# Spatial mixing by 26 block products of 4x4 blocks instead of seven of 2x2 blocks

## The chip, the cores and the metric

The kernel runs on one core of a Trainium2 chip. The metric is the device time of one execution in microseconds (us). Five engines work side by side, each in the order in which its instructions were written: PE multiplies matrices, DVE works on vectors, ACT applies functions and copies, POOL is a second, slower vector engine, and SP issues most of the DMAs (ACT issues those of the output). The profile adds PEld, the loading of PE's stationary operand, which overlaps PE.

## The reference, cut to what matters

One transformer block of 2048 tokens (S) and 448 channels (D): attention with 16 heads, then a gated MLP whose gate mixes the tokens. All data is float32.

```
h = layernorm(x) * (1 + ca) + sa
x = x + ga * attention(h)                 # 16 heads of 28 channels
h = layernorm(x) * (1 + cb) + sb
z = gelu(h @ w_in)                        # 2048 x 1792
z1 = z[:, :896]
z2 = layernorm(z[:, 896:])
g[t, f] = sum_s w_sp[t, s] * z2[s, f] + b_sp[t]     # the spatial mixing, 2048 x 2048 by 2048 x 896
x = x + gb * ((z1 * g) @ w_out)           # w_out: 896 x 448
```

The change concerns the line of `g`, and what prepares and consumes it.

## The kernel before

**Numbers and tiles.** A float32 matrix product is made of three matmuls in the format fp32r: each operand is split into a high part (an ACT copy) and a low part (a DVE subtraction), and high times high, high times low and low times high are summed in PSUM. In the mixing the stationary operand is a piece of z2 (128 tokens by 128 channels) and the moving one a piece of the transposed weights `w_spT` (128 source tokens by 512 target tokens). The 896 channels are seven tiles of 128, numbered f = 0 to 6. A matmul fills one PSUM bank with 128 channels by 512 targets.

**The mixing** (main loop L1420 to L1439). Targets, sources and channels 0 to 767 are halved, so that the mixing is a 2x2 by 2x2 block product, and it is done with seven block products instead of eight, at the price of sums of blocks. Two products make one phase, so there are four phases `p` (the last holds one product); each has two halves of the targets of a product, and each half eight steps `st` of 128 sources, which makes 64 steps. `mix_step` (matmuls L1250 to L1252) issues in one step three channel tiles of the first product, three of the second and the seventh channel tile, into seven of the PSUM ring's banks, where the sums grow over the eight steps of a half. `evac` then reads all seven banks, by ACT copies where an output is written first (L1262, L1275, L1282) and by DVE additions through `d_add` (L1255).

**Sums of weight blocks** come early. During attention 80 slots of its schedule (L818 to L825) hold the loading of two blocks by SP (`ws_load`), their sum on POOL (`ws_add`, L791) and its store to DRAM (`ws_store`, into `ws_scr`). Attention goes through 256 units of a head and a block of queries; slot n stands before unit n. In attention POOL also multiplies the heads' outputs by reciprocals of the softmax sums (L710) and prepares row maxima (L648, L649, L84), which PE transposes (`mtp`, L655).

**Sums of z2** are made by `z_sum` (L1143), some on POOL, some on DVE. The parts of the stationary operands are split per source tile by `prep0` to `prep3` (L1146 to L1162, L1227), into `heapA` and `heapB`.

**Order around it.** Nothing reorders instructions: the main loop writes them, and each engine takes its own in that order. `w_load` (L1125) fetches a weight tile some steps ahead into a pool of four buffers (`raw_sp`), `w_split` (L1133) splits it one or two steps ahead (`wsp_h` by ACT at L1138, `wsp_l` by DVE at L84). `extras` (L1364) lays the rest into the steps: the z parts, then `gate` (L1311: DVE adds the bias and multiplies by z1), `u_split` (L1322, the gated output into high and low parts `uT`), and the weights of the output projection (`wout_gate`, `wout_part`). `y_part` (L1350, matmuls L1356 to L1358) is the projection: 16 tiles of 128 tokens with 21 matmuls each. Tiles 8 to 11 stand inside the last half, tiles 12 to 15 and 0 to 7 behind the mixing. Before all this, `z2_gemm` (L1170) computes z2 tile by tile.

L84 before, and L141 after, is the line of the helper `sub`, which makes every low part on DVE or POOL.

Of the kernel before, what the change touches and what calls it, by code (L numbers as in the profile page):

```python
# [19 lines left out]
NT = S // 128  # L20
NG = 4

# [11 lines left out]
def tile_adaln_mha_gmlp(ctx, tc, x, wqkv, wo, w_in, w_spT, b_sp, w_out, cT, w_mod, out):  # L34
# [13 lines left out]
    ws_scr = scr.tile([80, 128, 512], F32, name="ws_scr")  # L48
# [22 lines left out]
    class Halves:  # L71
# [5 lines left out]
        def __getitem__(self, key):  # L77
            p, b, c = key
            return self.views[b // self.n][p, b % self.n, c]
# [675 lines left out]
    def win_first(i):  # L755
# [9 lines left out]
    SUMS = (  # L765
        ((0, 1), (1, 1), ALU.subtract),
        ((1, 0), (0, 0), ALU.subtract),
        ((0, 0), (1, 1), ALU.add),
        ((0, 0), (0, 1), ALU.add),
        ((1, 0), (1, 1), ALU.add),  # L770
    )

    def w_block(rc, st, half):
        rb, cb = rc
        return w_spT[(rb * 8 + st) * 128 : (rb * 8 + st + 1) * 128, (2 * cb + half) * 512 : (2 * cb + half + 1) * 512]
# [3 lines left out]
    def ws_tiles(i):  # L779
        if not ws_raw:  # L780
            ws_raw.append(dpool.tile([128, 7, 512], F32, name="ws_raw", tag="heapF"))
        return [ws_raw[0][:, 2 * (i % 3) + j, :] for j in range(2)]

    def ws_load(i):
        k, j = divmod(i, 16)
        for t, rc in zip(ws_tiles(i), SUMS[k]):
            sp.dma_start(t, w_block(rc, j // 2, j % 2))

    def ws_add(i):
        a, b = ws_tiles(i)  # L790
        pool.tensor_tensor(out=a, in0=a, in1=b, op=SUMS[i // 16][2])  # L791

    def ws_store(i):
        sp.dma_start(ws_scr[i], ws_tiles(i)[0])
# [116 lines left out]
    heapA = fh.tile([128, 8 * 896], F32R, name="heapA")  # L911
    heapB = fh.tile([128, 8 * 896], F32R, name="heapB")
    xl3 = fh.tile([128, 7, 512], F32, name="xl3", tag="heapC")
    w1 = hview(heapA, 0, 8, 896)
    h2T = [hview(heapB, g * 3584, 7, 512) for g in range(2)]

    zst = [(heapA, heapB)[i // 4][:, i % 4 * 1792 : (i % 4 + 1) * 1792] for i in range(8)]
# [185 lines left out]

    wp = ctx.enter_context(tc.tile_pool(name="wp", bufs=4))  # L1110
    F1, F2, F6, FQ = slice(0, 384), slice(384, 768), slice(768, 896), slice(384, 896)

    PHASES = (("s", 0, (1, 1)), ("s", 1, (0, 0)), ("s", 2, 3), ("s", 4, None))
    steps = [(p, half, st) for p in range(4) for half in range(2) for st in range(8)]

    def w_sources(p, half, st):
        _, k, q = PHASES[p]
        res = [ws_scr[k * 16 + st * 2 + half]]
        if q is not None:
            res.append(ws_scr[q * 16 + st * 2 + half] if isinstance(q, int) else w_block(q, st, half))  # L1120
        return res[::-1] if p == 3 else res

    raws, wsp = {}, {}

    def w_load(n):  # L1125
        if n < len(steps) and n not in raws and n not in wsp:
            raws[n] = []
            for src in w_sources(*steps[n]):
                t = wp.tile([128, 512], F32, name="raw_sp")
                sp.dma_start(t, src)  # L1130
                raws[n].append(t)

    def w_split(n):  # L1133
        if n < len(steps) and n not in wsp:
            wsp[n] = []
            for raw in raws.pop(n):
                hi = wp.tile([128, 512], F32R, name="wsp_h")
                act.activation(hi, raw, AF.Copy)  # L1138
                lo = wp.tile([128, 512], F32R, name="wsp_l")
                sub(dve, lo, raw, hi)  # L1140
                wsp[n].append((hi, lo))

    def z_sum(dst, a, b, op=ALU.add, eng=pool):  # L1143
        eng.tensor_tensor(out=dst, in0=a, in1=b, op=op)

    def z_part(hi, lo, src):  # L1146
        act.activation(hi, src, AF.Copy)
        sub(dve, lo, src, hi)

    def prep0(st):  # L1150
        h, l = zst[st][:, 0:896], zst[st][:, 896:1792]
        z_part(h[:, F1], l[:, F1], z2[st][:, F1])
        z_part(h[:, F2], l[:, F2], z2[8 + st][:, F1])
        z_part(h[:, F6], l[:, F6], z2[8 + st][:, F6])

    def prep1(st):
        h, l = zst[st][:, 0:896], zst[st][:, 896:1792]
        z_part(h[:, F1], l[:, F1], z2[8 + st][:, F2])
        z_part(h[:, FQ], l[:, FQ], z2[st][:, FQ])

    def prep2(st):
        z_part(zst[st][:, 0:896], zst[st][:, 896:1792], z2[st])  # L1162

    zt = [dpool.tile([128, 8 * 896], F32, name=f"z2{i}", tag=f"heapD{i}") for i in range(2)]
    z2 = [zt[i // 8][:, i % 8 * FH : (i % 8 + 1) * FH] for i in range(NT)]
    ph4 = ExitStack()
# [20 lines left out]
    def z2_norm(t):  # L1187
        mv, rs = z_mv.pop(t)
        dve.tensor_scalar(out=z2[t], in0=z2[t], scalar1=mv[:, 0:1], scalar2=rs, op0=ALU.subtract, op1=ALU.mult)
        if t >= 8:  # L1190
            z_sum(z2[t][:, F1], z2[t][:, F1], z2[t - 8][:, F1])

    for t in range(NT + 1):
        if t < NT:
            z2_gemm(t)
        if 0 < t <= NT:
            z2_norm(t - 1)
        if t in (10, 11, 14, 16):
            w_load((10, 11, 14, 16).index(t))
        if t in (13, 15):  # L1200
            w_split(t // 15)
        if 10 <= t < NT:
            prep0(t - 10)
# [4 lines left out]
    cE = fh.tile([128, 4 * 896], F32, name="cE", tag="heapE")  # L1208
    cC = fh.tile([128, 4 * 896], F32, name="cC", tag="heapC")
    cF = dpool.tile([128, 4 * 896], F32, name="cF", tag="heapF")  # L1210
    cD = dpool.tile([128, 4 * 896], F32, name="cD", tag="heapD2")
    u11, u12, u21, u22 = ([c[:, i * 512 : (i + 1) * 512] for i in range(6)] for c in (cE, cC, cF, cD))

    dq = [c[:, 3072:3584] for c in (cE, cC)]
    u6 = [c[:, 3072:3584] for c in (cF, cD)]

    def utile(f, tb):
        if f == 6:
            return (dq, u6)[tb // 2][tb % 2]
        return ((u11, u12), (u21, u22))[f // 3][tb // 2][2 * (f % 3) + tb % 2]  # L1220

    wouts_h, wouts_l = (hview(heapB, i * 3136, 7, D) for i in range(2))
    z7l = t4.tile([128, 256], F32R, name="z7l", bufs=1)
    z7 = [(heapA[:, i * 1024 : i * 1024 + 768], heapA[:, i * 1024 + 768 : i * 1024 + 1024]) for i in range(7)]
    z7.append((heapB[:, 6272:7040], z7l))

    def prep3(st):  # L1227
        a, b = z7[st]
        z_part(a[:, 0:384], a[:, 384:768], z2[8 + st][:, F1])
        z_part(b[:, 0:128], b[:, 128:256], z2[8 + st][:, F6])  # L1230

    def stationary(p, st, i):

        if p < 3:
            return zst[st][:, i * 128 : (i + 1) * 128], zst[st][:, 896 + i * 128 : 896 + (i + 1) * 128]
        a, b = z7[st]
        if i < 3:
            return a[:, i * 128 : (i + 1) * 128], a[:, 384 + i * 128 : 384 + (i + 1) * 128]
        return b[:, 0:128], b[:, 128:256]

    acc = {}

    def mix_step(n):
        p, half, st = steps[n]
        for i in (range(7) if p < 3 else (0, 1, 2, 6)):
            if st == 0:
                acc[i] = bank("acc")
            hi, lo = wsp[n][0 if i < 3 else -1]
            zh, zl = stationary(p, st, i)
            pe.matmul(acc[i], zh, hi, start=st == 0, stop=False)  # L1250
            pe.matmul(acc[i], zh, lo, start=False, stop=False)  # L1251
            pe.matmul(acc[i], zl, hi, start=False, stop=st == 7)  # L1252
        del wsp[n]

    def d_add(dst, a, b, op=ALU.add):  # L1255
        dve.tensor_tensor(out=dst, in0=a, in1=b, op=op)  # L1256

    def evac(p, x):
        for f in range(3):
            i = 2 * f + x  # L1260
            if p == 0:
                act.activation(u22[i], acc[f], AF.Copy)  # L1262
            elif p == 1:
                act.activation(u21[i], acc[f], AF.Copy)
                d_add(u11[i], u11[i], acc[f])
            elif p == 2:
                d_add(u11[i], u11[i], acc[f])
                d_add(u22[i], u22[i], acc[f])
            else:
                d_add(u11[i], u11[i], acc[f])  # L1270
        for f in range(3):
            i = 2 * f + x
            if p == 0:
                d_add(u12[i], u22[i], acc[3 + f])
                act.activation(u11[i], acc[3 + f], AF.Copy, scale=-1.0)  # L1275
            elif p == 1:
                d_add(u21[i], u21[i], acc[3 + f])
                d_add(u22[i], u22[i], acc[3 + f], ALU.subtract)
# [208 lines left out]
```

## Time and profile before

| what | us |
|---|---|
| median of 3 runs (1395.46 to 1396.77) | 1396.19 |
| span of the profiled execution | 1394.6 |
| up to the mixing (start of its first matmul) | 1050.3 |
| mixing and output projection | 344.3 |
| DVE busy in attention's window (170 to 975) | 629.1 of 805 |
| DVE, ACT and POOL busy in the last 344.3 us | 217.7, 120.6, 32.7 |

The three runs' median is 1.6 us above the span of the execution that was profiled; stages and durations are from that execution. The window from 170 to 975 us holds attention and the projections up to z1, that from 975 to 1050.3 the product that gives z2. A row of a window lists its length and then, for each engine, busy time and the number of instructions; a row of the groups lists line, engine, operation, output and inputs, their shapes, the count, the busy time, the mean duration in ns, and the idle time of that engine ahead of them with what ended it. A row of the timeline gives start, duration, engine, line, operation, and in square brackets how long it waited and for what.

### The profile page before, as it was taken

How to read it: one execution, taken by the hardware profiler on the slowest of the kernel's cores; microseconds unless marked ns; L12 is line 12 of the kernel's file. 1: busy time of each engine (PE TensorE's matmuls, PEld its weight loads, DVE VectorE, ACT ScalarE, POOL GpSimd, SP SyncE). 2: the span in 40 equal slices, each digit the busy share in tenths (PEclk: the TensorE clock that was granted, in tenths of full speed). 3: DMA queues.
4: the chain of work that ended last, by engine and by line, in shares of the span. 5: the costliest groups of instructions: out<-in, count | busy, mean ns of one | idle time of the engine just before them, and what ended most of it. 6: DMA issues, size and time to landing. Idle time of an engine off the chain costs nothing.

```text
span 1394.6 us, 20350 instructions
## 1 busy us (share of the span) xinstructions
PE 1389.6 (100%) x7192; PEld 991.3 (71%) x7192; DVE 1028.3 (74%) x1741; ACT 777.0 (56%) x1490; POOL 282.7 (20%) x306
## 2 busy tenths in 40 slices
PE   9999999999999999999999999999999999999999
PEld 8888655555555555555555555988998888888888
DVE  8798888888888888888888851850366655768574
ACT  5623677777766666777777779363234544434211
POOL 2234212222224143313200021000142330000000
PEclk9999999999999999999999999999999999999999
DMA  8565634555455546555322002433103333444453
GB/s 266 149 178 181 192 109 152 175 173 155 149 173 175 158 161 184 167 158 153 113 68 76 21 18 68 166 123 139 48 4 111 112 110 111 143 137 163 142 171 113
DMA packets 99377, 187.01 MB, mean 134 GB/s; under 512 B 17736, under 2 KB 29130, under 8 KB 96730
## 3 DMA queue, kind: packets, MB, share of 16 engines
q1 hardware_dynamic: 96558, 181.42, 42.4%
q10 hardware_dynamic: 2718, 4.30, 0.8%
q8 instruction: 56, 0.92, 0.3%
q14 instruction: 45, 0.37, 0.1%
HBM read 130.42 MB, written 50.46 MB: 130 GB/s over the span
## 4 chain that ended last, share of the span: by engine, by line
PE 99%; DMA 0%; DVE 0%; ACT 0%; ACTq 0%; issue 0%
PE st_ps L666 19%; PE o_ps L681 17%; PE mt L634 17%; PE acc L1250 7%; PE acc L1252 7%; PE acc L1251 7%; PE z_ps L1176 5%; PE pq L323 5%; PE z_ps L1062 5%; PE wo_ps L928 3%; PE pv L305 2%; PE y_ps L1357 2%; PE y_ps L1358 2%; PE y_ps L1356 2%; PE tp L117 1%; PE pv L477 1%
## 5 line engine op out<-in xcount | busy, mean ns | idle before, releaser
L639 DVE TENSOR_REDUCE pm<-mt 128x1 f32<-128x512 f32 x1024 | 631.3, 682 | 86.0 <-PE mt L634 85.9
L670 ACT ACTIVATE P<-st_ps 128x512 f32<-128x512 f32 x1024 | 514.7, 632 | 201.8 <-PE st_ps L666 201.7
L666 PE MATMUL st_ps<-qst,kst 128*128 128x512 f32 x1024 | 404.5, 406 | 0.0
L634 PE MATMUL mt<-kst,qst 128*128 128x512 f32 x1024 | 402.4, 393 | 0.0
L666 PEld LDWEIGHTS st_ps<-qst,kst 128*128 128x128 f32 x1024 | 191.2, 188 | 141.4 <-issue 93.1
L681 PE MATMUL o_ps<-P,V 128*32 128x512 f32 x2048 | 247.1, 598 | 0.0
L634 PEld LDWEIGHTS mt<-kst,qst 128*128 128x128 f32 x1024 | 192.4, 188 | 31.6
L791 POOL TENSOR_TENSOR ws_raw<-ws_raw 128x512 f32<-128x512 f32 x80 | 102.9, 1287 | 298.5 <-DMA ws_raw<-in_w_spT_dram 295.7
L1138 ACT ACTIVATE wsp_h<-raw_sp 128x512 fp32r<-128x512 f32 x112 | 70.0, 631 | 153.6 <-PE acc L1252 102.4
L681 PEld LDWEIGHTS o_ps<-P,V 128*32 128x32 f32 x2048 | 54.7, 109 | 123.0 <-issue 114.7
L84 DVE TENSOR_TENSOR wsp_l<-raw_sp,wsp_h 128x512 fp32r<-128x512 f32 x112 | 80.6, 729 | 81.9 <-ACT wsp_h L1138 81.2
L1250 PE MATMUL acc<-wsp_h,heapA 128*128 128x512 f32 x224 | 87.3, 390 | 0.0
L1251 PE MATMUL acc<-wsp_l,heapA 128*128 128x512 f32 x224 | 87.2, 389 | 0.0
L1252 PE MATMUL acc<-wsp_h,heapA 128*128 128x512 f32 x224 | 87.2, 389 | 0.0
L1251 PE MATMUL acc<-wsp_l,heapB 128*128 128x512 f32 x174 | 67.7, 389 | 0.0
L1250 PE MATMUL acc<-wsp_h,heapB 128*128 128x512 f32 x174 | 67.7, 389 | 0.0
L1252 PE MATMUL acc<-wsp_h,heapB 128*128 128x512 f32 x174 | 67.7, 389 | 0.0
L323 PE MATMUL pq<-heapD,heapD 128*128 128x512 f32 x196 | 61.9, 390 | 0.0
L1180 DVE BATCH_NORM_STATS2 stz<-z 128x6 f32<-128x448 f32 x32 | 19.9, 625 | 50.4 <-ACT z L1179 30.0
L1250 PEld LDWEIGHTS acc<-wsp_h,heapA 128*128 128x128 f32 x224 | 42.1, 188 | 8.9 <-DVE cD L1256 0.3
L1252 PEld LDWEIGHTS acc<-wsp_h,heapA 128*128 128x128 f32 x224 | 42.0, 188 | 8.8
L1251 PEld LDWEIGHTS acc<-wsp_l,heapA 128*128 128x128 f32 x224 | 42.0, 188 | 8.6
(224 smaller groups left out, 1598.8 us busy)
## 6 DMA issues: line engine op xcount, KB each, us to landing
ws_raw<-in_w_spT_dram SPq DMA_DIRECT2D x160, 256.0 KB
ws_scr<-ws_raw SPq DMA_DIRECT2D x80, 256.0 KB
raw_sp<-ws_scr SPq DMA_DIRECT2D x80, 256.0 KB
kst<-qk_scr SPq DMA_DIRECT2D x45, 224.0 KB
qst<-qk_scr SPq DMA_DIRECT2D x45, 224.0 KB
raw_sp<-in_w_spT_dram SPq DMA_DIRECT2D x32, 256.0 KB
qk_scr<-qh SPq DMA_DIRECT2D x28, 256.0 KB
qk_scr<-ql SPq DMA_DIRECT2D x28, 256.0 KB
```

The lines of the kernel that those rows point to most:

```text
L84: eng.tensor_tensor(out=dst, in0=a, in1=hi.bitcast(F32), op=ALU.subtract)
L323: pe.matmul(pq, wqk[:, b, m * 128 : (m + 1) * 128], hT[g][:, a, :], start=j == 0, stop=j == NST - 1)
L634: pe.matmul(mt, qst[h % 3][:, t * 128 : (t + 1) * 128], kst[h % 3][:, kb * 512 : (kb + 1) * 512], start=True, stop=True)
L639: dve.tensor_reduce(out=pms[h][:, t, kb : kb + 1], in_=mt, axis=AX.X, op=ALU.max)
L666: pe.matmul(st, kst[h % 3][:, kt * 128 : (kt + 1) * 128], qst[h % 3][:, qb * 512 : (qb + 1) * 512], start=True, stop=True)
L670: act.activation(p, st, AF.Exp, scale=SCALE)
L681: pe.matmul(otile[h][32 * qb : 32 * qb + 32, :], V[:, kt, h, :], ptiles.pop((u, qb)), start=kt == 0, stop=kt == NT - 1)
L791: pool.tensor_tensor(out=a, in0=a, in1=b, op=SUMS[i // 16][2])
L1138: act.activation(hi, raw, AF.Copy)
L1250: pe.matmul(acc[i], zh, hi, start=st == 0, stop=False)
L1251: pe.matmul(acc[i], zh, lo, start=False, stop=False)
L1252: pe.matmul(acc[i], zl, hi, start=False, stop=st == 7)
```

## The change

The mixing becomes 26 block products of 4x4 source and target blocks of 512 tokens. A product takes a combination of weight blocks (512 sources by 512 targets) and a combination of z2 blocks (512 sources by 384 channels), four steps of 128 sources. Three channel tiles belong to a product; the 768 channels are two blocks of three tiles (`A`: f = 3 to 5, `B`: f = 0 to 2), hence 2x4 by 4x4. The seventh tile (f = 6) rides with 16 of the products as a fourth tile. Each product's row in `PRODUCTS` says with which signs it enters the outputs (four blocks of targets of `A`, with f = 6, then four of `B`), whether f = 6 is in it, whether it starts a new chain, and which block of the weights it uses directly (`None`: a combination from `ws_scr`).

In a chain the PSUM banks are not cleared: a product is added to what its banks hold from the product before it in the same set. Products use the two sets (n even, n odd) in turn. After a product only those outputs read the running sum whose sign changes at that place (function `coef`); 28 reads write an output first and are ACT copies, 77 are DVE additions.

The sums of weights are listed in `W_SUMS`, slot by slot, with seven buffers: `0=w14.0` loads, `2=0+1` adds on POOL, `-2` negates on POOL, `p15.0=2` stores, `3=p20.0` loads a stored one again. There are 124 additions, 20 negations, 72 loads of weights, 12 of stored sums and 92 stores; before there were 80, 0, 160, 0 and 80. Sums of z2 move to DVE and take four source tiles in one instruction, as do the high parts (`z_hi`, ACT) and low parts (`z_low`, DVE). Bias and gate move from DVE to POOL, but for those written into `rest`. All 16 tiles of the output projection stand behind the mixing. Matmuls of the mixing: 1128 for 1200.

```diff
+PRODUCTS = [
+    ("0000000-", False, True, None),
+    ("0+0-0000", True, True, 1),
+    ("0000++-0", False, True, None),
+    ("-0+0+0-0", False, True, None),
+    ("0000+000", False, False, 0),
...
+W_SUMS = (
+    "2:0=w14.0,1=w13.0 3:3=w2.0 5:2=0+1,-2 6:4=w15.0,0=3-0,p15.0=2 7:5=w11.0,2=1-0,p14.0=0 8:p16.0=2 9:0=4+1 "
...
+    def ws_op(op):
+        if op[0] == "p":
...
+            sp.dma_start(ws_scr[4 * n + st], ws_tile(i))
+        elif op[0] == "-":
...
+            pool.tensor_scalar(out=t, in0=t, scalar1=-1.0, scalar2=None, op0=ALU.mult)
+        elif op[2] in "wp":
...
+            sp.dma_start(ws_tile(op[0]), w_block(n, st) if op[2] == "w" else ws_scr[4 * n + st])
+        else:
+            pool.tensor_tensor(
...
-    for i, slot in enumerate([j for j in range(2, 190, 2) if j % 16 != 12][:80]):
-        at(slot, ws_load, i)
-        at(slot + 3, ws_add, i)
-        at(slot + 5, ws_store, i)
+    for entry in W_SUMS.split():
...
-        at(200 + 8 * i, win_first, i)
+        at(204 + 8 * i, win_first, i)
...
+    def z_op(out, a, b, op=ALU.add):
+        dve.tensor_tensor(out=out, in0=a, in1=b, op=op)
...
+    def z_hi(n, *srcs):
...
+            act.activation(zhi[n % 3][:, :, c], s, AF.Copy)
...
+    def z_low(n):
+        for c, s in zsrc.pop(n):
+            sub(dve, zlo[n % 3][:, :, c], s, zhi[n % 3][:, :, c])
...
+    SUMS = {
+        4: lambda: [(ZS, ZA[0], ZB[2]), (ZS, ZS, ZB[0])],
+        5: lambda: [(ZS, ZA[0], ZT[0])],
...
+    def z_begin(n):
+        for s in SUMS[n]() if n in SUMS else ():
+            z_op(*s)
+        if n in HIS:
+            z_hi(n, *HIS[n]())
...
+    def mix_step(i):
+        n, st = mix[i]
...
+        for j in range(4 if six else 3):
+            start = st == 0 and (first6[n] if j == 3 else new)
...
+            for k, (z, w) in enumerate(((zh, hi), (zh, lo), (zl, hi))):
+                pe.matmul(
+                    a[j], z[:, c], w, start=start and k == 0, stop=st == 3 and k == 2, skip_group_check=not new or j == 3
...
+    def read(u, a, r, key):
+        if key not in written:
+            written.add(key)
+            act.activation(u, a, AF.Copy, scale=float(r))
+        else:
+            d_add(u, u, a, ALU.add if r > 0 else SUB)
...
+    def bias(f, k, eng=pool):
+        d_add(utile(f, k), utile(f, k), bt[k], eng=eng)
...
+    gates(20, 3, B3, 3, gate)
+    gates(21, 1, A4, 3, z1_load)
+    gates(22, 0, A4, 3, gate)
+    gates(22, 1, B3, 3, u_split)
...
+    for i, (n, st) in enumerate(mix):
+        w_load(i + 5)
+        w_load(i + 4)
+        w_split(i + 3 if i else 3)
+        if st == 0 and n:
+            todo += read_list(n - 1)
+        mix_step(i)
+        if st == 1:
+            z_begin(n + 2) if n + 2 not in (2,) else None
+        for _ in range(3):
+            if todo:
+                read(*todo.pop(0))
+        if st == 3:
+            z_end(n + 2) if n + 2 not in (2,) else None
+        for fn, a in extra.pop((n, st), []):
+            fn(*a)
...
+    last = [12, 13, 14, 15] + list(range(12))
...
+    for k, t in enumerate(last):
...
+        y_part(t)
+        for fn, *a in rest.get(k, ()):
+            fn(*a)
```

How the order of the instructions changes is shown at three places. First the reading of the banks. Before, on ACT at the end of the first half of phase 0, it stands in one piece; `cD` and `cE` are output buffers, `acc` a PSUM bank:

```order
L1262 ACTIVATE cD<-acc 128x512 x3
L1275 ACTIVATE cE<-acc 128x512 x3
L1282 ACTIVATE cE<-acc 128x512
L1138 ACTIVATE wsp_h<-raw_sp 128x512 x4
L1147 ACTIVATE heapA<-z_10937 128x384
```

After, on ACT in products 2 and 3, which read the banks of products 1 and 2; `cC` too is an output, `cE` here the sum of z2 blocks for product 4:

```order
L1409 ACTIVATE cC<-acc 128x512
L1409 ACTIVATE cD<-acc 128x512
L1409 ACTIVATE cC<-acc 128x512
L1170 ACTIVATE wsp_h<-raw_sp 128x512
L1203 ACTIVATE heapA<-cE 128x4x384
L1409 ACTIVATE cD<-acc 128x512
L1409 ACTIVATE cC<-acc 128x512
L1409 ACTIVATE cD<-acc 128x512
L1170 ACTIVATE wsp_h<-raw_sp 128x512
L1409 ACTIVATE cC<-acc_11625 128x512
L1409 ACTIVATE cD<-acc_11625 128x512
L1170 ACTIVATE wsp_h<-raw_sp 128x512 x2
```

The reads now stand in groups of up to three per step between the splits, and the high part of the z2 sum for the product after next (L1203) stands ahead of three to five of them.

Second, POOL in one head of attention. Before, from one row maximum to the next:

```order
L791 TENSOR_TENSOR ws_raw<-ws_raw 128x512 x5
L710 TENSOR_TENSOR osb<-osb,rb 128x512
L791 TENSOR_TENSOR ws_raw<-ws_raw 128x512 x2
L648 TENSOR_SCALAR mxv<-mxv 128x16
L649 CAST mxp<-mxv 128x16
```

After, a head in the same place of the program:

```order
L845 TENSOR_TENSOR ws_raw<-ws_raw 128x512 x4
L840 TENSOR_SCALAR ws_raw<-ws_raw 128x512
L845 TENSOR_TENSOR ws_raw<-ws_raw 128x512
L840 TENSOR_SCALAR ws_raw<-ws_raw 128x512
L845 TENSOR_TENSOR ws_raw<-ws_raw 128x512 x2
L767 TENSOR_TENSOR osb<-osb,rb 128x512
L845 TENSOR_TENSOR ws_raw<-ws_raw 128x512 x3
L705 TENSOR_SCALAR mxv<-mxv 128x16
```

Ten sums or negations stand where seven sums stood, and three instead of two of them between the normalisation (`osb`) and the row maximum (`mxv`).

Third, DVE and POOL in products 22 and 23, where nothing comparable stood before. DVE (`uT` is the split of gated outputs, `cE`, `cC` are outputs that read a bank):

```order
L1392 TENSOR_TENSOR cE<-cE,acc 128x512 x3
L141 TENSOR_TENSOR wsp_l<-raw_sp,wsp_h 128x512
L1193 TENSOR_TENSOR z_10936<-z_10936 128x4x384
L1392 TENSOR_TENSOR cE<-cE,acc_12874 128x512
L141 TENSOR_TENSOR uT<-cD,uT 128x512
L141 TENSOR_TENSOR wsp_l<-raw_sp,wsp_h 128x512
L141 TENSOR_TENSOR uT<-cD,uT 128x512
L141 TENSOR_TENSOR wsp_l<-raw_sp,wsp_h 128x512
L141 TENSOR_TENSOR heapA<-z_10936,heapA 128x4x384
```

POOL in the same stretch, where `bt` is a bias and the numbered `z` a tile of z1:

```order
L1392 TENSOR_TENSOR cD<-cD,z_13232 128x512
L1392 TENSOR_TENSOR cF<-cF,bt 128x512
L1392 TENSOR_TENSOR cD<-cD,z_13252 128x512
L1392 TENSOR_TENSOR cF<-cF,bt 128x512
L1392 TENSOR_TENSOR cD<-cD,z_13273 128x512
L1392 TENSOR_TENSOR cF<-cF,bt 128x512
```

The gates and biases that stood on DVE now stand on POOL, one or two for each step of the mixing.

More of the change, by code (lines that the diff above doesn't have):

```diff
@@ L1110, in tile_adaln_mha_gmlp @@
     wp = ctx.enter_context(tc.tile_pool(name="wp", bufs=4))
[L1111 to L1121, printed above, removed]
@@ L1123, in tile_adaln_mha_gmlp @@
-    raws, wsp = {}, {}
[L1125 to L1141, printed above, removed]
@@ L1209, in tile_adaln_mha_gmlp @@
[L1209 to L1220, printed above, removed]
@@ L1222, in tile_adaln_mha_gmlp @@
[L1222 to L1278, printed above, removed]
[L1279 to L1286 removed]
+    us += [fh.tile([128, 4 * 896], F32, name="cC", tag="heapC")]
@@ new lines, in zb, with d_add, read_list @@
+    def zb(n):
+        return 1 if n == NP - 1 else n % 3
+    def d_add(dst, a, b, op=ALU.add, eng=dve):
+        eng.tensor_tensor(out=dst, in0=a, in1=b, op=op)
+    written = set()
+    def read_list(n):
+        res = []
+        for j in range(4):
+            for o, r, six in reads[n]:
+                if six != (j == 3):
+                    continue
+                f, k = (3 + j if o < 4 else j), o % 4
+                res.append((utile(f, k), acc[n % 2][j], r, (f, k)))
+        return res
```

511 lines of the change are left out of this document (308 added, 203 removed).

## The prediction

> **What bounds the kernel now.** I read the page's busy times, its slices and its chain first, then the span cut into stages.
>
> ```profile
> span 1394.6 us, 20350 instructions
> ...
> PE 1389.6 (100%) x7192; PEld 991.3 (71%) x7192; DVE 1028.3 (74%) x1741; ACT 777.0 (56%) x1490; POOL 282.7 (20%) x306
> ...
> PEclk9999999999999999999999999999999999999999
> ...
> PE 99%; DMA 0%; DVE 0%; ACT 0%; ACTq 0%; issue 0%
> ```
>
> PE is on the chain for 99% of the span at full granted clock, so time can be won only by taking instructions from PE, and lost only by making it wait. But a busy share is a poor witness, because pipelined matmuls overlap. The stages, and two 20 us pieces of the spatial mixing, show it better:
>
> ```profile
> 170.00:975.00 805.00, 805.00 (x4445) 493.27 (x4445) 629.14 (x1081) 547.35 (x1067) 171.69 (x185) 1.00 0.44 132
> 1050.30:1394.60 344.30, 340.79 (x1537) 288.04 (x1535) 217.66 (x340) 120.61 (x215) 32.74 (x29) 1.00 0.41 132
> ...
> 1150.00:1170.00 20.00, 20.00 (x90) 16.54 (x90) 11.46 (x18) 7.23 (x12) 0.00 (x0) 1.00 0.28 90
> 1190.00:1210.00 20.00, 20.00 (x89) 16.29 (x88) 15.38 (x23) 8.96 (x15) 0.00 (x0) 1.00 0.48 144
> 1370.00:1394.60 24.60, 21.09 (x105) 19.20 (x103) 5.85 (x10) 1.19 (x3) 0.00 (x0) 1.00 0.25 84
> ```
>
> Columns after the window: its length, then busy time and count of PE, PEld, DVE, ACT and POOL, clock, DMA share, GB/s. The mixing and the output projection after it (second row) have only the 3.5 us tail in which PE is idle (24.60 less 21.09). The pace inside is read from the start of the first mixing matmul and that of the 673rd (phases 0 and 1 are 336 each), both in the timeline:
>
> ```profile
> 1050.30 0.39 PE L1250 MATMUL acc<-wsp_h,heapA 128*128 128x512 f32 x1
> ...
> 1202.63 0.39 PE L1250 MATMUL acc<-wsp_h,heapA 128*128 128x512 f32 x1
> ```
>
> 152.33 us over 672 is **0.2267 us a matmul**, without a gap. The 390 ns of a matmul's own duration is latency and prices nothing here.
>
> **The change part by part.** *Removed from PE.* Before: seven block products of 3 channel tiles, 16 steps and 3 matmuls (1008), and the seventh tile in four phases of 16 steps (192), 1200 in all. After: 26 x 3 x 4 x 3 = 936, and 16 x 4 x 3 = 192 for the seventh tile, 1128. 72 fewer at 0.2267 us: **-16.3 us**. The output projection keeps its 336 matmuls; 84 of them, tiles 8 to 11, move from inside phase 3 to behind the mixing, where tiles 12 to 15 come first, and their operands are finished in products 22 to 25. PE waited nowhere in this stretch but in its tail (above), so I cost the move at nothing.
>
> *Added beside PE.* A product has 36 or 48 matmuls, so 8.16 or 10.88 us (26 of them 255.7 us), in which the other engines must have split the weights, built the next product's stationary tiles and read the banks. Prices:
>
> ```profile
> L84 DVE TENSOR_TENSOR wsp_l<-raw_sp,wsp_h 128x512 fp32r<-128x512 f32 x112 | 80.6, 729 | 81.9 <-ACT wsp_h L1138 81.2
> L84 DVE TENSOR_TENSOR uT<-cD,uT 128x512 fp32r<-128x512 f32 x7 | 4.8, 684 | 0.0
> L84 DVE TENSOR_TENSOR heapA<-z,heapA 128x896 fp32r<-128x896 f32 x4 | 4.4, 1093 | 0.6
> L1144 DVE TENSOR_TENSOR z<-z,z 128x384 f32<-128x384 f32 x8 | 4.4, 550 | 0.0
> L1256 DVE TENSOR_TENSOR cE<-cE,acc 128x512 f32<-128x512 f32 x19 | 12.6, 683 | 0.9 <-PE acc L1252 0.9
> L1138 ACT ACTIVATE wsp_h<-raw_sp 128x512 fp32r<-128x512 f32 x112 | 70.0, 631 | 153.6 <-PE acc L1252 102.4 <-DVE x2t L1361 28.0 <-DMA raw_sp<-ws_scr 16.1
> L1147 ACT ACTIVATE heapA<-z 128x384 fp32r<-128x384 f32 x19 | 9.3, 511 | 0.0
> L1147 ACT ACTIVATE heapA<-z 128x896 fp32r<-128x896 f32 x4 | 3.8, 938 | 0.0
> L791 POOL TENSOR_TENSOR ws_raw<-ws_raw 128x512 f32<-128x512 f32 x80 | 102.9, 1287 | 298.5 <-DMA ws_raw<-in_w_spT_dram 295.7 <-PE mt L634 2.7
> ```
>
> The new z operations take 1536 or 2048 elements of a partition at once, which no row shows. From 384 (550 ns) to 896 elements (1093 ns) DVE adds 1.06 ns an element: 1.77 and 2.31 us, estimates. Bounds: one 896 operation, 1.09, from below, four of 384, 2.2, from above. ACT by its two rows: 1.47 and 1.90 us. I use these, being on the line through both rows. DVE then has 104 splits (71.1 at 684 ns), 73 reads of banks (49.9), z lows (47.5), z sums (38.8), uT and wouts (9.2): 217 us in 255.7, 85%. ACT has about 130. So no engine replaces PE on average; what counts is where the load bunches.
>
> *Bunch one, products 2 to 4.* The 28 first reads are ACT's, and products 1 and 2 have 14 of them. ACT runs in order, and the row of the z high part stands ahead of later reads and waits for sums on DVE. Reads out of PSUM on ACT come at 0.62 us each:
>
> ```profile
> 1087.35 1.96 ACT L1275 ACTIVATE cE<-acc 128x512 f32<-128x512 f32 x3 [0.87 <-DVE cC L1256]
> 1089.20 0.59 ACT L1282 ACTIVATE cE<-acc 128x512 f32<-128x512 f32 x1
> ```
>
> Walk it from the start of product 2 (time 0). ACT: a split to 0.9, three reads to 2.75, a split to 3.4. DVE: its low part to 4.1, two sums of 1.77 for product 4 to 7.6. ACT: z high to 9.1, three reads to 9.7, 10.3 and 10.95, a split to 11.6. PE begins product 3 at 8.16 in the bank set that product 1 used; its second tile needs the read of 9.7 instead of 8.84 (0.9 lost), its third that of 10.95 (0.55), its second step a low part of 12.3 (0.45). Then ACT: two reads, two splits, three reads and a split, to 16.5. DVE: z low to 15.9, two lows to 17.25, a sum to 19.0. ACT: two z highs to 21.1 and reads to 21.7 and 22.95. PE is at the second tile of product 4 at 18.9 and waits till 21.7 (2.8), then 0.55 and, for the next split, 0.4. Together **+5.6 us**; with sums at 1.09 about 3, at 2.2 about 7.5. Behind product 4 the reads are three on DVE, the next product has 10.88 us, and ACT catches up.
>
> *Bunch two, products 22 to 25.* In 22 and 23 DVE has 8 splits, 8 reads, a sum, a z low, 7 uT and 3 wouts: 5.5 + 5.5 + 3.5 + 4.8 + 1.9 = 21.2 in 21.8 us. POOL now does biases and gates, 13 operations there (27 through 25, 56 from product 10 on), and DVE and POOL disturb each other:
>
> ```profile
> 1099.85 1.15 DVE L84 TENSOR_TENSOR heapA<-z,heapA 128x384 fp32r<-128x384 f32 x2
> ...
> 1108.96 1.98 DVE L84 TENSOR_TENSOR heapA<-z,heapA 128x384 fp32r<-128x384 f32 x2
> ...
> 1125.54 1.87 DVE L1256 TENSOR_TENSOR cC<-cD,acc 128x512 f32<-128x512 f32 x3
> ...
> 1107.47 2.44 POOL L1144 TENSOR_TENSOR z<-z,z 128x384 f32<-128x384 f32 x2
> 1125.76 1.02 POOL L1144 TENSOR_TENSOR z<-z 128x384 f32<-128x384 f32 x1 [1.17 <-DVE heapB L84]
> ```
>
> The same pair takes 1.15 alone and 1.98 beside POOL: 0.83 more in a step with three POOL operations, about 0.3 each. A read from PSUM beside POOL is not longer (1.87 for three). So DVE falls 13 x 0.3 = 4 us late, at 0.83 each 11. A split is issued three steps ahead, 8.2 us, of which it needs 1.3 itself; the cover is 6.8. I take **+1.5**, between nothing and 4.
>
> The page "SBUF — State Buffer" of the Trainium skill, section "Who interferes with whom", says that a VectorE instruction with two SBUF inputs and a GpSimd one exclude each other for a whole instruction, and that one SBUF input doesn't contend; the rows above agree in kind, and by it alone each POOL operation could cost its whole length (rival 2).
>
> *Attention.* POOL gets 124 sums and 20 negations for 80 sums, between slots 2 and 200 (575 us); 160 us plus 12 to 26 (as the cast of 0.61 or as a sum). Per head two to four stand between the normalisation and the row maximum that PE's transpose needs. Before, that chain ends at 412.07, the transpose comes at 413.30, and POOL had been the cause of PE's wait twice:
>
> ```profile
> 410.91 0.22 DVE L646 TENSOR_REDUCE mxv<-pm 128x16 f32<-128x64 f32 x1
> 411.85 0.22 POOL L84 TENSOR_TENSOR mxp<-mxv,mxp 128x16 fp32r<-128x16 f32 x1
> 413.30 0.09 PEld L655 LDWEIGHTS mtp<-ident,mxp 128*32 128x32 f32 x1 [0.84 <-issue]
> ...
>   POOL ws_raw L791: 1.7, 2
> ```
>
> The two adds before it ended 2.9 us early (POOL waited that long for DVE), so a third fits: 0. SP issues 176 transfers there for 240, hence nothing later. If that cover goes it is rival 3. Mixing loads are 104 for 112; z2's DVE work stays alike (13 us of new z work for 12 us of old). Nothing there is priced.
>
> Sum, against this execution's span: 1394.6 - 16.3 + 5.6 + 1.5 = 1385.4. The median of the runs is 1.6 above the span, and I keep that: **1387.0 us**.
>
> **Rivals.** *1, the cover holds:* ACT's early reads overlap better than 0.62 and the sums are nearer 1.1, PE never waits: 1394.6 - 16.3 + 1.6 = 1379.9. For it: before, PE was paced at 0.2267 straight through the bank changes at 1088 and 1203. Against: those had seven banks in a ring and no sum in ACT's way. *2, POOL stops DVE:* from product 10 on DVE has 139 us in PE's 160.5. With the full 1.287 for each of 56 POOL operations it needs 211, 44 more than PE and the cover of 6.8, and the time is 1431, slower than before. It turns slower where an operation costs DVE more than 39.6 / 56 = 0.7 us (160.5 - 139 + 6.8 and the 10.7 won); at 0.45 the stalls are local, about 1391. The rows say 0.3. That whole-instruction lock is the page's rule just named; the trace has seen it for one operation in three. *3, sums on POOL delay the transpose:* two sums of 1.287 behind each other, less 1.23 of slack, 1.34 for each of 12 heads, 16: 1403. Against: POOL waits for DVE there. *4, the change doesn't do what it says:* excluded, PE's order has 1128 mixing matmuls for 1200 and is otherwise equal in number.
>
> **How the numbers follow.** Forecast 0.65 (1383 to 1391), rival 1 0.15, rival 2 0.12, rival 3 0.08. The range takes the forecast, rival 1 and the mild half of rival 2: 1379.5 to 1393.5. A measurement tells 0.2%, 2.8 us, from no change: faster than 1393.4 are forecast, rival 1 and 0.05 of rival 2, 0.85; within, 0.04 of rival 2 and 0.02 of rival 3, 0.06; slower, the rest of both, 0.09.
>
> **What would show it.** Mixing matmuls 1128 at 0.2267 and a first-to-last stretch of 256 us plus gaps; gaps of 0.5 to 3 us at the second and third tiles of products 3 and 4, ended by ACT reads (bunch one wrong if PE runs through there); a gap of a microsecond or two behind product 22, ended by DVE's low part (rival 2 if several, with two-input DVE rows near 1.5 us); attention still ending at the same time (rival 3 if later). It would be wrong altogether if matmuls that go on accumulating in a bank that is being read in between ran at another pace, of which no row tells.

## The result and the profile after

| | median, us | runs |
|---|---|---|
| before | 1396.35 | 1395.46 to 1396.77 |
| changed kernel | 1406.28 | 1404.25 to 1407.99 |

The changed kernel takes 1.0072 times as long, with an interval of 1.0057 to 1.0086: it is slower by some 10 us where 9 us less were forecast, and lies outside the forecast range. The profiled execution is the longest of its four, 1407.99 us with a span of 1406.1.

The page of the changed kernel, in the same parts as before (span, busy times, clock by slices, chain):

```profile
span 1406.1 us, 20080 instructions
...
PE 1384.8 (98%) x7120; PEld 978.5 (70%) x7120; DVE 1073.5 (76%) x1685; ACT 785.3 (56%) x1458; POOL 427.2 (30%) x394
...
PEclk9999999999999999999999999999999999999999
...
PE 7%; DVE 2%; issue 1%; DMA 1%; POOL 1%; ACT 0%; SPq 0%; DVEq 0%; ACTq 0%
```

PE is less busy by 4.8 us, and the span is longer by 11.5. The chain was followed back through some 12% of the span only, and in that piece PE holds little more than half, where it held 99% of the whole before. So PE now waits at the end, and the stages say where. The windows of the changed kernel, with the columns of the prediction's second fence; the second row is the mixing, from its first matmul to the first of the projection, the next two are products 10 to 17 and 18 to 25 of it, cut at the start of the first matmul of each, and the last is the projection:

```profile
170.00:975.00 805.00, 805.00 (x4448) 493.89 (x4447) 630.29 (x1083) 548.15 (x1069) 254.09 (x247) 1.00 0.38 111
1050.70:1334.37 283.67, 268.91 (x1130) 212.99 (x1128) 229.84 (x247) 119.01 (x175) 90.35 (x59) 0.98 0.39 123
1152.58:1237.13 84.55, 81.63 (x350) 64.86 (x348) 74.75 (x82) 34.91 (x45) 30.41 (x18) 1.00 0.40 123
1237.13:1334.37 97.24, 88.32 (x362) 68.87 (x360) 79.87 (x85) 33.04 (x49) 54.46 (x36) 0.96 0.44 140
1334.37:1406.10 71.73, 68.25 (x337) 62.91 (x335) 28.83 (x48) 11.28 (x21) 0.79 (x1) 1.00 0.37 120
```

Attention is untouched: POOL is busy 254.1 us there for 171.7, and the mixing starts at 1050.70 for 1050.30. The mixing's 1128 matmuls at 0.2267 us need 255.7 us and take 283.7, so **28.0 us are lost in it**. Products 10 to 17 are 348 matmuls, 78.9 us, and take 84.55: 5.7 lost. Products 18 to 25 are 360, 81.6 us, and take 97.24: 15.6 lost. From the starts of single matmuls, another 1.7 us are lost in product 0 and 5.0 in products 3 and 4, and nothing in the rest of the first ten. The account: 28.0 lost less 16.3 saved is 11.7, and 11.5 was added to the span.

DVE in the mixing after product 10, two groups of the changed kernel (shape apart; the window is 1152.6 to 1334.2), first the low parts of the weights, then the reads of banks into one of the outputs:

```profile
L141 DVE TENSOR_TENSOR wsp_l<-raw_sp,wsp_h 128x512 fp32r<-128x512 f32 x63 | 60.5, 974 | 22.6 <-ACT wsp_h L1170 22.6
...
L1392 DVE TENSOR_TENSOR cC<-cC,acc 128x512 f32<-128x512 f32 x21 | 13.4, 676 | 0.0
```

The instruction with two inputs in SBUF takes 0.97 us, where it took 0.70 in products 0 to 9 (40 of them); the one that reads PSUM takes 0.68, as in the kernel before. And DVE, at 75 to 80 us in each of the two stretches, also stands idle 22.6 us for ACT. One such place, at the start of product 10, in the timeline of the changed kernel (DVE, ACT, POOL, PE):

```profile
1149.87 0.97 DVE L141 TENSOR_TENSOR wsp_l<-raw_sp,wsp_h 128x512 fp32r<-128x512 f32 x1
1150.76 2.84 DVE L1193 TENSOR_TENSOR z<-z 128x1536 f32<-128x1536 f32 x1
1155.67 1.29 DVE L141 TENSOR_TENSOR wsp_l<-raw_sp,wsp_h 128x512 fp32r<-128x512 f32 x2 [2.07 <-ACT wsp_h L1170]
...
1153.63 1.49 ACT L1203 ACTIVATE heapA<-z 128x1536 fp32r<-128x1536 f32 x1 [8.33 <-DVE z L1193]
1155.03 2.18 ACT L1170 ACTIVATE wsp_h<-raw_sp 128x512 fp32r<-128x512 f32 x4
...
1148.99 5.76 POOL L1392 TENSOR_TENSOR cE<-cE,bt 128x512 f32<-128x512 f32 x3 [95.01 <-DVE cE L1392]
...
1155.69 0.50 PE L1384 MATMUL acc<-wsp_h,heapA 128*128 128x512 f32 x1 [0.23 <-ACT wsp_h L1170]
1156.41 0.50 PE L1384 MATMUL acc<-wsp_l,heapA 128*128 128x512 f32 x1 [0.22 <-DVE wsp_l L141]
```

Read it from DVE. The z sum takes 2.84 us beside POOL's biases, where it takes 1.75 alone. ACT has waited 8.33 us for it, since the high part of this sum is its next instruction, and four weight splits stand behind. When the sum is done, ACT makes the high part and the splits, DVE meanwhile has nothing and waits 2.07, and PE, whose split weights have run out, waits for both.

Three theories came out of this. **A**: POOL's biases and gates stretch DVE's instructions until DVE is too full. **B**: the order is at fault, the high part ahead of the weight splits. **C**: another wait behind POOL, such as loads held on SP's queue. PE's lost time is what the experiments are read by, always in the same way: the time of a stretch less its matmuls at 0.2267 us.

### The profile page after: what moved, and what is told of

The parts are those of the page before. It is cut to its first block, busy times and chain, and to the rows that moved or that the text cites. A ratio compares the mean times of both kernels' runs of the same rounds, so it can differ in the third digit from the quotient of the medians.

```text
span 1406.1 us, 20080 instructions
## 1 busy us (share of the span) xinstructions
PE 1384.8 (98%) x7120; PEld 978.5 (70%) x7120; DVE 1073.5 (76%) x1685; ACT 785.3 (56%) x1458; POOL 427.2 (30%) x394
## 5 line engine op out<-in xcount | busy, mean ns | idle before, releaser
L1384 PE MATMUL acc<-wsp_h,heapA 128*128 128x512 f32 x752 | 239.4, 397 | 6.9 <-ACT wsp_h L1170 3.5
L845 POOL TENSOR_TENSOR ws_raw<-ws_raw 128x512 f32<-128x512 f32 x124 | 159.2, 1287 | 192.8 <-DMA ws_scr<-ws_raw 128.6
L1384 PEld LDWEIGHTS acc<-wsp_h,heapA 128*128 128x128 f32 x752 | 143.3, 191 | 42.3 <-ACT wsp_h L1170 7.0
L1384 PE MATMUL acc<-wsp_l,heapA 128*128 128x512 f32 x376 | 150.0, 399 | 7.9 <-DVE wsp_l L141 7.8
L1384 PEld LDWEIGHTS acc<-wsp_l,heapA 128*128 128x128 f32 x376 | 71.8, 191 | 28.3 <-DVE wsp_l L141 14.0
L1203 ACT ACTIVATE heapA<-z 128x1536 fp32r<-128x1536 f32 (+2 forms) x25 | 33.7, 1359 | 54.9 <-DVE z L1193 53.3
L767 POOL TENSOR_TENSOR osb<-osb,rb 128x512 f32<-128x512 f32 x15 | 19.3, 1288 | 122.1 <-DMA rb<-r_scr 112.4
L1281 ACT ACTIVATE z<-z_ps 128x448 f32<-128x448 f32 x32 | 17.4, 545 | 47.2 <-PE z_ps L1278 47.2
L1392 POOL TENSOR_TENSOR cE<-cE,bt 128x512 f32<-128x512 f32 x7 | 12.2, 1767 | 99.1 <-DVE cE L1392 99.1
L141 DVE TENSOR_TENSOR heapA<-z,heapA 128x1536 fp32r<-128x1536 f32 (+2 forms) x25 | 42.0, 1689 | 0.0
```

The lines of the kernel that those rows point to most:

```text
L141: eng.tensor_tensor(out=dst, in0=a, in1=hi.bitcast(F32), op=ALU.subtract)
L845: pool.tensor_tensor(out=ws_tile(op[0]), in0=ws_tile(op[2]), in1=ws_tile(op[4]), op=ALU.add if op[3] == "+" else ALU.subtract)
L1203: act.activation(zhi[n % 3][:, :, c], s, AF.Copy)
L1384: pe.matmul(a[j], z[:, c], w, start=start and k == 0, stop=st == 3 and k == 2, skip_group_check=not new or j == 3)
```

## The experiments

All times in us; the ratio is to the kernel before, run on the same chip beside them.

| kernel | time | ratio, interval | lost in product 0 | 3 and 4 | 10 to 17 | 18 to 25 |
|---|---|---|---|---|---|---|
| changed kernel | 1406.28 | 1.0072 (1.0057 to 1.0086) | 1.7 | 5.0 | 5.7 | 15.6 |
| e1_no_gates | 1385.99 | 0.9918 (0.9902 to 0.9935) | 1.7 | 5.1 | 0.0 | 0.0 |
| e2_hi_later | 1395.34 | 0.9984 (0.9974 to 0.9993) | 1.7 | 0.0 | 0.0 | 13.3 |
| e3_gates_dve | 1410.12 | 1.0091 (1.0076 to 1.0106) | 1.7 | 3.6 | 6.7 | 18.6 |
| e4_tail_gates | 1395.82 | 0.9985 (0.9976 to 0.9995) | 1.7 | 3.7 | 6.2 | 2.7 |
| e5_hi_and_tail | 1381.89 | 0.9898 (0.9882 to 0.9915) | 1.7 | 0.0 | 0.0 | 0.0 |
| e6_first_product | 1380.90 | 0.9894 (0.9880 to 0.9909) | 0.8 | 0.0 | 0.0 | 0.4 |
| e7_wout_loads | 1404.71 | 1.0061 (1.0046 to 1.0076) | 1.7 | 3.7 | 5.9 | 13.5 |
| e7_hi_wout_loads | 1392.12 | 0.9970 (0.9959 to 0.9981) | 1.7 | 0.0 | 0.0 | 11.0 |
| e8_gates_aside | 1409.62 | 1.0098 (1.0083 to 1.0113) | 1.7 | 3.7 | 7.1 | 18.1 |
| e8_hi_gates_aside | 1399.32 | 1.0021 (1.0011 to 1.0030) | 1.7 | 0.0 | 1.8 | 15.6 |

### The biases and gates left out

```diff
     def bias(f, k, eng=pool):
+        if eng is pool:
+            return
...
     def gate(f, k, eng=pool):
-        d_add(utile(f, k), utile(f, k), z1s.pop((f, k)), ALU.mult, eng=eng)
+        z = z1s.pop((f, k))
+        if eng is dve:
+            d_add(utile(f, k), utile(f, k), z, ALU.mult, eng=eng)
```

> The 49 biases and gates that POOL does during the mixing are left out, with nothing in their place. In the changed kernel PE stands still for 20.7 us in products 10 to 25 and 6.4 us before. Theory A (POOL stretches DVE's instructions, 25 us in products 10 to 25, and DVE is then too full): the low parts of the weights fall from 0.97 to 0.70 us, the stalls of products 10 to 25 to under 3 us, the time to about 1388. Theory B (the order: on ACT the high part of a z sum stands ahead of weight splits and waits for DVE): the low parts get shorter too, but ACT still waits 5 us or more at several products, stalls of 10 us or more stay, about 1396. The stalls of products 0 to 4 stay 6.4 by both.

Theory A's numbers came: 1385.99 us, and products 10 to 25 lose nothing at all. The windows of products 10 to 17 and 18 to 25 in this run, and its low parts of weights:

```profile
1152.18:1231.06 78.88, 78.88 (x349) 65.36 (x348) 64.50 (x81) 35.25 (x45) 0.00 (x0) 1.00 0.42 131
1231.06:1312.66 81.60, 81.60 (x362) 67.61 (x360) 64.11 (x86) 33.33 (x49) 9.61 (x7) 1.00 0.52 167
...
L141 DVE TENSOR_TENSOR wsp_l<-raw_sp,wsp_h 128x512 fp32r<-128x512 f32 x63 | 42.8, 690 | 30.8 <-ACT wsp_h L1170 30.4
```

DVE does the same instructions in 128.6 us (64.50 and 64.11) that took 154.6 beside POOL (74.75 and 79.87). These are times in which DVE is busy, an overlap of neighbouring instructions counted once; the 139 us of the prediction and the 165 of the expectations add up the rows and come out some 10 us higher. Two of the 49 operations ran ahead of this stretch in the changed kernel, so the price is read from the first matmul of the mixing to the end of the kernel, changed kernel first:

```profile
1050.70:1406.10 355.40, 337.16 (x1465) 275.90 (x1463) 258.66 (x294) 130.28 (x196) 91.14 (x59) 0.99 0.39 123
```

```profile
1050.21:1384.38 334.17, 327.78 (x1465) 275.21 (x1463) 231.82 (x295) 131.24 (x196) 11.50 (x10) 0.99 0.41 130
```

DVE is busy 26.8 us less: **26.8 us for 49 POOL operations, 0.55 us each**. This run alone doesn't say whether POOL's use of the memory or the waits for its results cost the time, as both are gone.

### The order alone

```diff
         for s in SUMS[n]() if n in SUMS else ():
             z_op(*s)
+
+    def z_mid(n):
         if n in HIS:
             z_hi(n, *HIS[n]())
...
+        if st == 2:
+            z_mid(n + 2) if n + 2 not in (2,) else None
         if st == 3:
             z_end(n + 2) if n + 2 not in (2,) else None
```

> Only the order changes: the high part of a z sum is issued one step after the sum, behind that step's reads, not right behind the sum. POOL's work is as in the changed kernel. Theory A: DVE stays as long, 165 us of work in products 10 to 25; the stalls there stay within 4 us of 20.7, the time 1400 to 1406. Theory B: gaps ended by ACT's weight splits vanish, products 10 to 25 lose under 8 us, products 3 and 4 under 2.5 for 4.8, the time is about 1391.

Neither theory holds alone. Products 3 and 4 and 10 to 17 lose nothing now, as B has it, and 18 to 25 still lose 13.3, as A has it; the time is 1395.34. The windows of products 10 to 17 and 18 to 25:

```profile
1147.91:1226.84 78.93, 78.93 (x350) 65.28 (x348) 74.18 (x81) 33.75 (x44) 28.62 (x17) 1.00 0.42 128
1226.84:1321.73 94.89, 87.14 (x362) 67.85 (x361) 81.66 (x85) 33.57 (x49) 56.54 (x36) 0.98 0.45 145
```

DVE's work is stretched by POOL in both. In the first DVE has 74.2 us of work for PE's 78.9, and this order carries it without a gap; in the second it has 81.7 for PE's 81.6, so that any idle time of DVE there makes PE late.

### The gates on DVE again

```diff
-    def bias(f, k, eng=pool):
+    def bias(f, k, eng=dve):
...
-    def gate(f, k, eng=pool):
+    def gate(f, k, eng=dve):
```

> Biases and gates of the mixing and the seven products with the modulation (56 operations) back on DVE, at the same places. DVE in products 10 to 25 then has 139 + 56 x 0.68 = 177 us without a stretch, where it has 165 now. Theory A: each POOL operation cost DVE 0.46, so DVE has 12 us more, the time is about 1418, with low parts of 0.70. If POOL's help cost DVE nothing and the order alone stalls PE (B): 38 us more on DVE, 1440 or so.

The seven products with the modulation stayed on POOL, so 49 operations moved and not 56. The time, 1410.12, is nearer to A's 1418 than to B's 1440, and hits neither. From the first matmul of the mixing to the end, with all 49 in:

```profile
1050.41:1408.46 358.05, 337.40 (x1465) 276.09 (x1463) 264.89 (x343) 130.61 (x196) 10.54 (x10) 0.98 0.39 122
```

DVE is busy 264.9 us, 33.1 more than without the gates, or 0.67 for each operation. On POOL the same operation cost DVE 0.55 in the changed kernel, and 0.62 in e2_hi_later (262.2 us busy in the same stretch). So POOL relieved DVE of a fifth of this work at most.

### The gates beside the projection

Biases and gates of 25 operations leave products 18 to 25; the projection's tiles take them (the whole edit also moves loads and `u_split` into `rest`).

```diff
-    gates(18, 0, B3, 2, bias)
...
-    gates(18, 3, B3, 2, gate)
-    gates(20, 0, B3, 1, bias)
...
-    gates(23, 2, A4, 0, gate)
...
-    gates(22, 0, A4, 2, bias)
-    gates(24, 0, A4, 1, bias)
...
-    gates(25, 0, A4, 1, gate)
...
+        0: [(z1_load, f, 0, True) for f in A4] + [(bias, f, 1) for f in F7] + [(u_split, f, 0) for f in B3] + [(gate, f, 0, dve) for f in A4] + [(z1_load, f, 1, True) for f in B3],
...
+        4: [(bias, f, 2) for f in F7] + [(u_split, f, 1) for f in F7],
```

> 25 of POOL's 56 operations leave products 18 to 25: their biases and gates are done beside the output projection (14 biases on POOL, 11 gates more on DVE), where DVE is busy 29 of 72 us. Theory A: DVE gets back 25 x 0.46 = 11.5 us in products 18 to 25, whose stalls fall from 15.2 to about 4; about 1395, the projection still 72 us. Theory B: the stalls behind product 18 fall by a few us only, about 1402.

A's number came (1395.82 for 1395): products 18 to 25 lose 2.7 us for 15.6, products 10 to 17 keep theirs, 3 and 4 lose 1.3 less (the clock, last section), and from the first matmul of the projection to the end it takes 72.1 us for 71.7. The profiled execution is the fastest of the ten, 1394.04 us, so the median run loses somewhat more.

### Both edits, and the first product

> Both edits together: the high part of a z sum one step later, and the 25 operations of POOL beside the output projection. If the two causes are separate and meet only in products 18 to 25, the stalls of products 3, 4 and 10 to 17 go with the order (10.7 us) and those of 18 to 25 nearly with both (15.7): under 2 us there, 1.7 in product 0, and the time is 1381 to 1384, below the kernel before. If POOL's stretching of DVE in products 10 to 17 stalls PE whatever the order, 5 us or more stay there, 1388.

1381.89 us, 0.9898 times the kernel before (0.9882 to 0.9915). The mixing and products 18 to 25 in this run:

```profile
1050.41:1307.81 257.40, 256.33 (x1129) 211.52 (x1128) 219.89 (x250) 121.51 (x175) 57.89 (x37) 1.00 0.41 125
1226.21:1307.81 81.60, 81.60 (x361) 67.57 (x360) 69.00 (x87) 33.93 (x49) 26.25 (x17) 1.00 0.44 134
```

Of the 28.0 lost us 1.7 are left, all in product 0, and 1394.6 - 16.3 + 1.7 = 1380.0 is the span of 1379.9. Products 3 and 4 lost by the order alone. In 10 to 17 order and stretching had to come together, as without either of them nothing is lost there; products 18 to 25 need both edits.

For product 0, two DVE instructions were put behind the first two steps of the mixing:

```diff
-        14: lambda: z_end(1),
-        15: lambda: z_op(ZT[0], ZB[1], ZB[2]),
...
+    put(0, 0, z_end, 1)
+    put(0, 1, z_op, ZT[0], ZB[1], ZB[2])
```

> As the one before, and the low part of product 1 (2.3 us on DVE) and a z sum (1.75 us) are moved from before the mixing to behind its first two steps. If these stand ahead of the second weight split and make PE wait in product 0, its 1.7 us go, and the time is about 1.5 us under the run before. If the splits are late for another reason (their loads), the 1.7 us stay.

Product 0 loses 0.8 for 1.7, but product 1 then loses 0.5 and the last one 0.4. The runs (1380.62 to 1383.25) overlap those of the one before (1381.68 to 1382.05): no gain that can be told. In this trace half of product 0's loss went with these two instructions; where the rest comes from stays open.

### Loads on SP's queue

Theory C rested on two rows of waits in the changed kernel, SP's queue in products 18 to 25 and ACT in products 10 to 25 (sum, times, longest):

```profile
SPq L1442 <- DVE wouts L141: 20.8, 5, 8.9
```

```profile
ACT heapA L1203 <- DVE z L1193: 50.9, 7, 10.3
...
ACT wsp_h L1170 <- DMA raw_sp<-ws_scr: 17.9, 6, 7.1
```

A load of projection weights waits up to 8.9 us for its buffer, and weight loads queue behind it.

```diff
     def wout_load(f):
+        if f > 1:
+            x2t["w", f] = x2t["k", f % 2]
+            return
...
+        x2t["k", f] = raw
```

> Order and POOL's work as in the changed kernel, but five of the seven loads of the output projection's weights are left out (tiles 2 to 6 use the rows of tiles 0 and 1), so that no such load waits on SP's queue for its buffer; there, 5 waits cost 20.8 us and ACT waited 17.9 us for weight loads behind them. Theory C (SP's queue, held by those loads, delays the weights in products 22 to 25): the 15.7 us of products 18 to 25 fall under 8 and the time to about 1397. Theory A (POOL stretches DVE): they stay within 3 us, the time 1403 to 1406. Products 3 to 17 keep their 10.7 us by both.

> The same five loads left out, with the high part of a z sum one step later. Without the loads' change that order left 13.3 us of stalls in products 18 to 25 and gave 1395.3. Theory C: under 4 us stay, the time is about 1385. Theory A: 10 us or more stay, 1392 to 1395.

Products 18 to 25 still lose 13.5 us for 15.6, and 11.0 for 13.3 with the other order. So that queue carries about 2 us at most, and A's numbers hold for the rest (1404.71 and 1392.12). With the changed kernel's order these 2 us are no more than its runs differ among themselves; with the other order the runs (1391.53 to 1392.72) lie clear below those of e2_hi_later (1393.59 to 1395.68).

### POOL's work without its results

```diff
     def bias(f, k, eng=pool):
+        if eng is pool:
+            d_add(bt[k], utile(f, k), bt[k], eng=pool)
+            return
...
     def gate(f, k, eng=pool):
-        d_add(utile(f, k), utile(f, k), z1s.pop((f, k)), ALU.mult, eng=eng)
+        z = z1s.pop((f, k))
+        if eng is pool:
+            b = bt.get(1, bt[k])
+            d_add(b, utile(f, k), b, eng=pool)
+            return
+        d_add(utile(f, k), utile(f, k), z, ALU.mult, eng=eng)
```

> POOL's 49 biases and gates run at their places and read the same outputs, but write into the bias tile, and no gate reads z1: nothing waits for them and no z1 buffer waits for POOL. The gated result is left out. Order as in the changed kernel. Theory A: what POOL does to DVE stays, so do 5 us or more in products 10 to 17 and 8 us or more in 18 to 25; about 1400 to 1405. If instead the waits for POOL's results were the cause, products 10 to 25 run with under 4 us, as with the gates left out, 1388.

> The same with the high part of a z sum one step later. Theory A: of the 13.3 us in products 18 to 25 8 us or more stay, 1390 to 1395. If waits for POOL's results (or z1 buffers) were the cause: under 3 us, 1384.

With nothing waiting for POOL's biases and gates, products 10 to 17 lose 7.1 us and 18 to 25 lose 18.1 (15.6 with the other order), somewhat more than in the changed kernel, and the times, 1409.62 and 1399.32, lie a few us above A's. It is POOL's running beside DVE, not the waits for what it makes. This separates what the first experiment left together. From the first matmul of the mixing to the end, e8_gates_aside has

```profile
1049.45:1407.39 357.94, 336.26 (x1465) 273.33 (x1463) 265.43 (x295) 130.32 (x196) 94.04 (x59) 0.99 0.39 122
```

so that an operation on POOL cost DVE 0.69 us, as much as on DVE itself. Loads of z1 on SP's queue, which waited 14.4 us for POOL in products 18 to 25 of e7_wout_loads, no longer wait for it here, and the loss stays. So theory C is left with its 2 us, though no run takes away the waits of both kinds of loads at once.

## Why the prediction was wrong, step by step

*What bounds the kernel, and the saving.* Right. PE alone set the end, 72 matmuls fewer save 16.3 us, and e5_hi_and_tail shows the saving: its mixing takes 257.40 us, the 255.7 of 1128 matmuls and product 0's 1.7. Banks read between two accumulations change nothing in the pace: 349 matmul records in 78.88 us.

*Bunch one.* Right in place and cause, and in size partly by luck. Forecast were 1.9 us at product 3 and 3.7 at product 4, waiting for reads on ACT behind a z sum's high part; lost were 1.1 and 3.9. In the changed kernel, PE at the second tile of product 4, and ACT ahead of it:

```profile
1088.78 1.49 ACT L1203 ACTIVATE heapA<-cE 128x1536 fp32r<-128x1536 f32 x1 [2.80 <-DVE cE L1193]
1090.17 0.61 ACT L1203 ACTIVATE heapA<-z 128x512 fp32r<-128x512 f32 x1
1090.69 0.58 ACT L1409 ACTIVATE cF<-acc 128x512 f32<-128x512 f32 x1
...
1091.32 0.50 PE L1384 MATMUL acc<-wsp_h,heapA 128*128 128x512 f32 x1 [1.65 <-ACT cF L1409]
```

e2_hi_later took the whole 5.0 away by moving the high part, so the cause is shown. Some of that size was not forecast, though: e4_tail_gates, whose products 3 and 4 are the same program, lost 3.7, and the difference is the clock (below). The waits alone cost 3.7 for the forecast 5.6. The z operations of 1536 elements took 1.75 us, 2048 took 2.28, for estimates of 1.77 and 2.31.

*Bunch two* is the step that failed: "I take **+1.5**, between nothing and 4", for products 22 to 25. These lost 14.0, and products 10 to 21, where the sum has nothing, another 7.3. The step held two errors. The first is the price of a POOL operation, taken as 0.3 us from a single pair of rows; measured over 49 it is 0.55. The rows beside that pair, DVE first, in the kernel before:

```profile
1105.96 0.68 DVE L84 TENSOR_TENSOR wsp_l<-raw_sp,wsp_h 128x512 fp32r<-128x512 f32 x1
1108.30 0.74 DVE L84 TENSOR_TENSOR wsp_l<-raw_sp,wsp_h 128x512 fp32r<-128x512 f32 x1 [1.67 <-ACT wsp_h L1138]
1108.96 1.98 DVE L84 TENSOR_TENSOR heapA<-z,heapA 128x384 fp32r<-128x384 f32 x2
...
1106.18 1.34 POOL L1144 TENSOR_TENSOR z<-z 128x384 f32<-128x384 f32 x1 [1.76 <-DVE heapA L84]
1107.47 2.44 POOL L1144 TENSOR_TENSOR z<-z,z 128x384 f32<-128x384 f32 x2
```

DVE stood idle from 1106.64 to 1108.30, and the pair, which began at 1108.96, met only the last of POOL's three operations. So one operation cost the 0.83 us, and dividing by three took in two that ran beside an idle DVE or a split hardly longer than 0.68. This suggests that an operation costs more where DVE is fuller, as it is in products 10 to 25; no run tried that alone. The second error is the cover, taken as 6.8 us for every split, from the distance in the program alone. But the splits pass through ACT behind the high parts, which wait for DVE's sums, so a DVE that is late makes ACT late and then waits for ACT itself: 22.6 us of waiting in a stretch in which DVE has 155 us of work for PE's 160.5. The prediction walked this chain for products 2 to 4, and did not ask for it again where DVE is fuller. In products 10 to 17 both errors were needed for a loss: e1_no_gates without the stretching and e2_hi_later with another order lose nothing there. In 18 to 25 the stretching does nearly all of it, as 13.3 of 15.6 us stay with the other order.

*Rival 2* was the case, by its mechanism. Its point of decision, 0.7 us for an operation, and its "at 0.45 the stalls are local, about 1391" were wrong for the same reason: they compared sums of DVE and PE over sixteen products. At 0.55 the sums still fit (155 in 160.5) and the kernel is slower by 10 us. (The sum behind 0.7, 160.5 - 139 + 6.8 + 10.7, is 39.0 and not 39.6, which changes nothing.) The sign it named came, several gaps ended by low parts, with rows of 1.10 us in products 18 to 25 and not near 1.5. The Trainium skill, page "SBUF — State Buffer", section "Who interferes with whom", has a VectorE instruction with two SBUF inputs contend with a GpSimd one that reads SBUF, and none with one SBUF input; the rows agree, 0.97 for 0.69 us on the first kind and 0.68 unchanged on reads of PSUM. A lock for POOL's full 1.29 us at each operation was not seen on the average.

*Left out of the sum* were product 0's 1.7 us (half of it went with a low part and a z sum that stood ahead of the second split), against "Nothing there is priced", and the halved clock.

*Right at nothing*: attention (rival 3), where POOL's 82 us more of work moved the start of the mixing by 0.4; the projection, 72 us behind the mixing. Rival 1, with no wait at all, was not reached by the changed kernel, but its 1379.9 is within 2 us of what e5_hi_and_tail gives.

## What to carry to other kernels

When work moves to an engine that shares memory with the busy one, price it by what it costs the busy one, here 0.55 to 0.69 us on DVE for an operation that costs DVE itself 0.67, and look for a stage in which that engine is idle: beside the output projection 25 of these operations cost 0.3 us together. Compare loads stretch by stage, not over the whole, and follow each engine's own order for an instruction that waits on the busy engine while the next step's inputs stand behind it. An edit that saves the bound engine's work should be tried again with its cover repaired before it is given up: the same 26 products are 1% faster with two moves.

## What the runs showed of the hardware

PE's granted clock halved behind some stalls. In the changed kernel, 1.6 us after the wait of 1.65 us at product 4:

```profile
1092.90:1096.20 3.30, 3.30 (x9) 2.39 (x8) 3.30 (x4) 2.79 (x4) 0.00 (x0) 0.50 0.46 146
```

Such a spell lasts 3.4 us in the changed kernel, and one of 6.8 us is in e3_gates_dve and one in e7_wout_loads. Its price is read from product 4, which loses 3.9 and 4.0 us with a spell (changed kernel, e1_no_gates) and 2.6 without (e4_tail_gates): 1.3 to 1.4 us. The changed kernel has three in its mixing, by this price about 4 of its 28 lost us, an estimate; the kernel before and e5_hi_and_tail have none there. Behind the same wait at product 4, of 1.65 to 1.68 us, e3_gates_dve, e4_tail_gates, e7_wout_loads and e8_gates_aside have no spell. So it does not follow every stall, and what decides was not tried. The Trainium skill, page "TensorE: Matmul & The Clock Gate", section "Why this matters for your kernels", warns of idle gaps over some 3 us between bursts of matmuls; here shorter ones were enough.
